# Attention scores from unsplit float32 operands, two heads on row halves, in place of split float32r products

## The chip, the cores and the metric

The kernel runs on one core of a Trainium2 chip. The metric is the device time of one execution in microseconds (us), the median of three runs. PE is TensorE, DVE is VectorE, ACT is ScalarE, POOL is GpSimd, SP is SyncE, which here only issues DMAs.

## What is computed

Attention with a soft cap, then two feed-forward networks, all in float32 from outside:

```python
# q, k, v: [2, 12, 448, 64]; cap = 30
scores = q @ k.T / 8
scores = cap * tanh(scores / cap)
attn = exp(scores - max(scores))
x = (attn / (sum(attn) + 1e-9)) @ v          # -> [896, 768]
h = x @ w_in                                 # [768, 2048]
x = max(0.01 * h, h) @ w_out                 # [2048, 768]
xn = x / sqrt(mean(x * x) + 1e-6) * rms_g
out = (silu(xn @ w_gate) * (xn @ w_val)) @ w_out2   # 768 -> 1536 -> 768
```

## The kernel before

The attention works on 12 pairs of heads (2 batches of 6 pairs). One tile `qk` of a pair holds, on 128 partitions, the 64 channels of both heads: 448 columns of queries (part "q"), 128 columns with the last 64 keys of both heads as two diagonal blocks (part "r"), and 384 columns with the first three blocks of 128 keys (part "k"). `scores` makes the scores of a pair in four units: the diagonal block "r" for both heads at once, with all 128 rows, and three units of one block of keys for each of the two heads. A head's keys and queries are on 64 partitions, so in these units each head uses one half of TensorE's rows.

Before, `split` gives `q` and `k` in two parts: `kqh` (float32r, rounded to 12 bits; cast on DVE, L453) and `kql = qk - kqh` (the helper at L345, on POOL, some on DVE). A score is then hi x hi + hi x lo + lo x hi. The first three pairs (0 to 2) do that with three products for each head, on row halves. For pairs 3 to 11 eight small DMAs on SP's queue (L478) also copy parts of both heads into `xq` and `xk`, so that hi x hi and lo x hi of a head are one product over all 128 rows (L509), and hi x lo stays a product on row halves (L499).

From the scores, ACT makes the tanh (L528) and the exponential (L536) into `e`. The weighted sums `weigh` are float32 products: one with all rows and columns (L547) for the last keys, then three units in which the two heads stand on halves of the columns (L550). For the denominator, `add_up` adds the blocks of `e` into `a` (L568 on DVE, L574 on POOL, then L581 for one head on POOL and for the other on DVE) and sums over the partitions on TensorE (L587, two float32 products on column halves). `finish` takes the reciprocal (L598), multiplies (L599) and splits the result into `xh` (L604, POOL) and `xl` (L345, DVE), the operands of the first network.

The order of instructions is written out beforehand. Every step is entered in a plan with an engine, an assumed cost in ns and a rank; the plan works through the steps in assumed time, takes on each engine the lowest rank among those that could start, and gives out the order found. Each engine then executes in that order and waits at semaphores where a step isn't ready. When TensorE has nothing ready in the plan, it gets a filler product (`warm`, L671, at most 18 calls). The 64-bit weights of the networks are decoded in the kernel into two float32r parts (`load_w`: DMA L380 on SP, ACT L383, DVE L387, L392 and twice L377, ACT L399, POOL or DVE L345); the first three blocks of `w_in` are decoded during the attention. The products of the first network (L710 for those blocks, then L795) can start when the last scores have been issued.

A step of TensorE's plan before, with its assumed cost, and the one of the weighted sums, which stays:

```python
plan.add("pe", (4 * MM, 0.75), r, across, reads, [(sc,)] + done)      # MM = 189 ns
...
plan.add("pe", 752 if i == 3 else 802, rank(h.n, "weigh"), product, reads, [(po,)])
```

Of the kernel before, what the change touches and what calls it, by code (L numbers as in the profile page):

```python
# [18 lines left out]
# Which engine does a step, how many buffers there are, and where kinds of steps stand (in hundredths of a pair)  # L19
# [3 lines left out]
    "kt": "2",  # L23
# [4 lines left out]
    "hk": "dve",  # L28
    "hq": "dve",
    "lk": "pool",  # L30
    "lq": "pool",
    "hk0": "dve",
    "hq0": "dve",
    "lk0": "pool",
    "lq0": "dve",
# [14 lines left out]
    "split": "-700",  # L50
    "low": "-130",
# [8 lines left out]
    "move": "-550",  # L60
    "load0": "-600",
    "load_v0": "-460",
    "split0": "215",
    "low0": "-670",
# [23 lines left out]
class Buf:  # L88
    """A tile that is taken from its pool where it is first written."""
# [15 lines left out]
class Fixed:  # L105
    """A tile that is there already."""
# [18 lines left out]
class Plan:  # L125
    """Steps with estimated costs, put in an order that keeps the engines busy."""
# [11 lines left out]
    def stretch(self, at, cost):  # L138
        """The time of a step of TensorE, whose clock is halved after a window with few matmuls."""
        cost, share, self.after = (*cost, 0) if isinstance(cost, tuple) and len(cost) == 2 else cost if isinstance(cost, tuple) else (cost, 1.0, 0)  # L140
        t = at
        while cost > 1e-6:
            tick = int((t + self.offset) / self.TICK + 1e-9)
            speed = 1.0 if self.seen.get(tick - 1, 0.0) >= self.ENTRY else 0.5
            step = min((tick + 1) * self.TICK - self.offset - t, cost / speed)
            self.seen[tick] = self.seen.get(tick, 0.0) + step * speed * 2.4 * share
            cost -= step * speed
            t += step
        return t - at
# [121 lines left out]
def softcap_attention_leaky_moe_gated_moe(  # L271
# [13 lines left out]
    """float32 products are carried as float32r pairs: x = hi + lo with hi = x rounded to 12 bits and  # L285
    lo = x - hi, which 12 bits hold exactly; x @ y = hi @ hi + hi @ lo + lo @ hi (+ lo @ lo where it
    rides along), every product exact and every sum in float32."""
# [27 lines left out]
    def scales():  # L315
        """|cap|, -|cap| and 1 / (|cap| sqrt(D))."""
        nc.vector.tensor_scalar_mul(ncap, cap_t, -1.0)
        nc.vector.tensor_max(acap, cap_t, ncap)
        nc.vector.reciprocal(tsc, acap)
        nc.vector.tensor_scalar_mul(tsc, tsc, SCALE)  # L320

    def network(ctx, bounded):
# [8 lines left out]
        def spare_w(i, part):  # L331
            """Room for one part of a block of a matrix in a spare block."""
# [17 lines left out]
        def load_w(src, hi=None, lo=None, rank=None):  # L350
            """A block of a float64 matrix (its words in src, [128, n]) as its two float32r parts.

            F, the upper word read as a float32, holds the upper eight exponent bits in its exponent; F * 2^-16
            moves the exponent's bias from float64's to float32's, the shift by three drops the sign and the
            exponent bits above float32's, and the three next bits of the fraction come from the lower word.
            Magnitudes outside of float32's range are clamped to it first."""
# [75 lines left out]
        def rank(n, kind):  # L432
            """Where steps of a kind for pair n stand among the steps that are ready."""
# [5 lines left out]
        def split(h):  # L439
            """q and k of a pair of heads, with the channels of both on the partitions, in their two parts."""  # L440
            raw, r = h.load["qk"], rank(h.n, "split")
            h.hi, h.lo = (Buf(st, [P, KW + QW], F32R, nm, 2) for nm in ("kqh", "kql"))
            alone = h.n < kn("n0", 2)
            for kind in ("q", "r", "k") if alone else ("q", "rk"):
                at = slice(parts_of[kind[0]].start, parts_of[kind[-1]].stop)
                n = at.stop - at.start
                eng = ENV["h" + kind + "0"] if alone else ENV["h" + kind[-1]]

                def upper(at=at, eng=eng):
                    if eng == "act":  # L450
                        nc.scalar.copy(h.hi[:, at], raw[:, at])
                    elif eng == "dve":
                        nc.vector.tensor_copy(h.hi[:, at], raw[:, at])  # L453
                    else:
                        nc.gpsimd.tensor_scalar(h.hi[:, at], raw[:, at], 1.0, 1.0, op0=ALU.mult, op1=ALU.mult)

                cost = {"act": cost_act(n), "dve": cost_dve(n, True), "pool": cost_pool(n, False)}[eng]
                plan.add(eng, cost, r, upper, [(raw, x) for x in kind], [(h.hi, x) for x in kind], [h.lo])
                eng = ENV["l" + kind + "0"] if alone else ENV["l" + kind[-1]]
                cost = {"dve": cost_dve(n), "pool": cost_pool(n, True)}[eng]  # L460
                plan.add(
                    eng, cost, rank(h.n, "low"),
                    lambda at=at, eng=eng: low(nc.vector if eng == "dve" else nc.gpsimd, h.lo[:, at], raw[:, at], h.hi[:, at]),
                    [(x, y) for x in (raw, h.hi) for y in kind], [(h.lo, x) for x in kind],
                )
            h.x = None
            if h.n < kn("n0", 2):
                return
            h.x = [Buf(st, [P, 2, m], F32R, nm, kn("xb", 2)) for nm, m in (("xq", KW), ("xk", 3 * P))]
            for j in range(2):  # L470
                own, other = (slice(i * D, (i + 1) * D) for i in (j, 1 - j))
                for i, (kind, to, src) in enumerate((("q", own, h.hi), ("q", other, h.hi), ("k", own, h.hi), ("k", other, h.lo))):
                    x = h.x[kind == "k"]
                    m = x.args[1][2]
                    at = slice(parts_of[kind].start, parts_of[kind].start + m)
                    plan.add(
                        "dma", [(650, 320 if kind == "q" else 274)], rank(h.n, "move"),
                        lambda x=x, to=to, j=j, src=src, own=own, at=at: nc.sync.dma_start(  # L478
                            x[to, j].bitcast(F32), src[own, at].bitcast(F32)
                        ),  # L480
                        [(src, kind)], [(x, j, i % 2)],
                    )

        def scores(h, at):
            """Some of the seven chunks of 128 keys: the soft cap of their scores, over |cap|."""
# [3 lines left out]
            stacked = h.x is not None and at[0] > 0  # L489
            hi, lo, queries = h.hi, h.lo, parts_of["q"]  # L490
# [5 lines left out]
            def products(terms, first, last):  # L496
                for m, (x, y) in enumerate(terms):
                    for j, rows in enumerate(rows_of):
                        nc.tensor.matmul(  # L499
                            sc[:, j, :S], x[rows, own], y[rows, queries],  # L500
                            start=first and m == 0, stop=last and m == len(terms) - 1,
                        )

            def across():
                xq, xk = h.x
                at = slice(c0 - parts_of["k"].start, c0 - parts_of["k"].start + P)
                products([(hi, lo)], True, False)
                for j in range(2):
                    nc.tensor.matmul(sc[:, j, :S], xk[:, j, at], xq[:, j], start=False, stop=True)  # L509

            done = [("scored",)] * (h.n == NPR - 1)
            share, r = 1.0 if at[0] == 0 else 0.5, rank(h.n, "score")
            if stacked:
                reads = [(hi, "k"), (lo, "q")] + [(x, j, k) for x in h.x for j in range(2) for k in range(2)]
                plan.add("pe", (4 * MM, 0.75), r, across, reads, [(sc,)] + done)
            else:
                terms = [(hi, hi), (hi, lo), (lo, hi)]
                groups = [(terms[:1], True, False), (terms[1:], False, True)] if h.n == 0 else [(terms, True, True)]
                for group in groups:
                    reads = {(x, kind) for x, _ in group[0]} | {(y, "q") for _, y in group[0]}  # L520
                    plan.add(
                        "pe", (len(group[0]) * len(rows_of) * MM, share), r,
                        lambda group=group: products(*group), sorted(reads, key=lambda v: (v[0] is lo, v[1])), [(sc,)] + done,
                    )
# [15 lines left out]
        def weigh(h, i):  # L540
            """One chunk of keys of each head: the heads are on halves of the columns, side by side."""
# [619 lines left out]
```

## Time and profile before

| | us |
|---|---|
| three runs | 645.37, 646.57, 647.38 |
| median | 646.57 |
| profiled execution, first to last instruction | 644.4 |
| TensorE busy in it | 619.7 (96%) |
| DVE busy | 493.3 (77%) |
| ACT busy | 270.5 (42%) |
| POOL busy | 240.7 (37%) |

Of the profiled execution only the span from its first to its last instruction is recorded; the timed runs lie 1.0 to 3.0 us above it. Busy time of TensorE is modelled, and its products overlap: the time from the start of one to the start of the next is the better measure of what a product costs. "Granted clock" is the share of full speed, 2.4 GHz, that TensorE's clock had.

### The profile page before, as it was taken

Reading aid. Unit: us, or ns where it says so; the run is one execution under the profiler, and the core shown is the slowest. Engines: PE = TensorE matmul, PEld = TensorE weight load, DVE = VectorE, ACT = ScalarE, POOL = GpSimd, SP = SyncE. Lnnn points to the kernel's source line nnn. Section 1 sums busy time; section 2 is a strip of 40 time slices with the busy share of each in tenths; the row PEclk is TensorE's granted clock in tenths of the full one; section 3 lists DMA queues with packets and bytes.
Section 4 is the critical chain, followed back from the end, with each engine's and each line's share of the span. In section 5 each row is a group of like instructions: output and inputs, shape, how many; then the busy total and the mean of one; then the engine's idle time right before and its main releaser. Section 6 shows DMA issues by size and latency. Waiting matters only on the chain.

```text
span 644.4 us, 7884 instructions
## 1 busy us (share of the span) xinstructions
PE 619.7 (96%) x2990; PEld 517.5 (80%) x2990; DVE 493.3 (77%) x577; ACT 270.5 (42%) x378; POOL 240.7 (37%) x150
## 2 busy tenths in 40 slices
PE   9988899999999999999999979999999999899996
PEld 6333333499999999998999869999999989899995
DVE  4999999989988885688866983998876269899110
ACT  6966777335545443333332442434333134333000
POOL 2867797612232222454353522333222034333100
PEclk9989999999999999999999989999999999999999
DMA  7566665122333323434344020343333022454110
GB/s 253 155 181 181 164 157 148 50 98 66 132 116 125 103 81 101 128 93 147 116 164 151 2 98 1 126 140 127 127 119 108 40 99 98 148 161 146 51 38 28
DMA packets 22719, 73.55 MB, mean 114 GB/s; under 512 B 3856, under 2 KB 10640, under 8 KB 22672
## 3 DMA queue, kind: packets, MB, share of 16 engines
q1 hardware_dynamic: 22672, 72.96, 35.8%
q8 instruction: 25, 0.41, 0.3%
q14 instruction: 22, 0.18, 0.1%
HBM read 62.52 MB, written 2.75 MB: 101 GB/s over the span
## 4 chain that ended last, share of the span: by engine, by line
PE 73%; DVE 14%; POOL 4%; DMA 3%; issue 3%; ACT 2%; SPq 1%; DVEq 0%; ACTq 0%; POOLq 0%
PE ps L795 32%; PE pt L795 15%; PE ps L840 15%; PE ps L1011 4%; DVE wm L377 3%; PE ps L888 3%; DVE rs L598 2%; PE sc L710 2%; DVE kqh L453 2%; DMA wraw<-in_moe_w_out_dram 2%; POOL kql L345 2%; DVE a L581 1%; DVE a L568 1%; PE pt L710 1%; DVE wm L387 1%
## 5 line engine op out<-in xcount | busy, mean ns | idle before, releaser
L377 DVE SCALAR_TENSOR_TENSOR wm<-wraw,wm 128x768 int32<-128x768 int32 (+1 forms) x140 | 168.4, 1203 | 2.8
L345 POOL TENSOR_TENSOR wlo<-wm,whi 128x768 fp32r<-128x768 f32 (+1 forms) x45 | 87.4, 1943 | 215.2 <-ACT whi L399 204.4
L383 ACT ACTIVATE wm<-wraw 128x768 f32<-128x768 f32 (+1 forms) x70 | 62.2, 889 | 127.3 <-DMA wraw<-in_moe_w_out_dram 54.9
L795 PE MATMUL ps<-low_g,whi 128*128 128x448 f32 x288 | 82.5, 367 | 0.0
L795 PE MATMUL ps<-low_g,spare 128*128 128x448 f32 (+1 forms) x330 | 67.7, 362 | 0.0
L387 DVE TENSOR_SCALAR wm<-wm 128x768 f32<-128x768 f32 (+1 forms) x70 | 44.4, 635 | 30.3 <-ACT wm L383 29.9
L795 PEld LDWEIGHTS ps<-low_g,spare 128*128 128x128 f32 x330 | 61.5, 188 | 4.6
L795 PEld LDWEIGHTS ps<-low_g,whi 128*128 128x128 f32 x288 | 54.1, 188 | 5.0
L795 PE MATMUL pt<-xl,whi 128*128 128x448 f32 x156 | 57.4, 368 | 0.0
L795 PE MATMUL pt<-xh,wlo 128*128 128x448 f32 x156 | 57.4, 368 | 0.0
L795 PE MATMUL pt<-xh,whi 128*128 128x448 f32 x156 | 57.4, 368 | 0.0
L345 DVE TENSOR_TENSOR high_g<-u,high_g 128x448 fp32r<-128x448 f32 x32 | 47.5, 1484 | 11.1 <-ACT high_g L641 9.7
L795 PE MATMUL ps<-low_g,wlo 128*128 128x448 f32 x144 | 53.1, 369 | 0.0
L528 ACT ACTIVATE e<-sc,tsc 128x896 f32<-128x896 f32 (+1 forms) x48 | 42.6, 910 | 21.6 <-PE sc L509 19.4
L392 DVE TENSOR_SCALAR wm<-wm 128x768 int32<-128x768 int32 (+1 forms) x70 | 46.8, 670 | 1.5
L399 ACT CAST whi<-wm 128x768 fp32r<-128x768 f32 (+1 forms) x45 | 36.4, 809 | 22.3 <-DVE wm L377 9.5
L840 PE MATMUL ps<-high_g,whi 128*128 128x448 f32 x152 | 43.6, 368 | 0.0
L840 PE MATMUL ps<-low_g,whi 128*128 128x448 f32 x152 | 43.6, 368 | 0.0
L536 ACT ACTIVATE e<-e,acap 128x896 f32<-128x896 f32 (+2 forms) x47 | 42.7, 957 | 0.0
L1072 DVE COPY o<-ps 128x384 f32<-128x384 f32 x14 | 7.6, 554 | 38.0 <-PE ps L795 38.0
L345 POOL TENSOR_TENSOR kql<-qk,kqh 128x448 fp32r<-128x448 f32 (+2 forms) x21 | 29.4, 1409 | 19.0 <-DVE kqh L453 18.6
L345 POOL TENSOR_TENSOR spare<-wm,spare 128x768 fp32r<-128x768 f32 x11 | 21.8, 1990 | 38.0 <-ACT spare L399 34.6
(154 smaller groups left out, 1232.2 us busy)
## 6 DMA issues: line engine op xcount, KB each, us to landing
wraw<-in_moe_w_out_dram SPq DMA_DIRECT2D x24, 768.0 KB, 4.5
wraw<-in_moe_w_in_dram SPq DMA_DIRECT2D x16, 768.0 KB, 4.4
wraw<-in_moe_w_gate_dram SPq DMA_DIRECT2D x12, 768.0 KB, 4.3
wraw<-in_moe_w_val_dram SPq DMA_DIRECT2D x12, 768.0 KB, 4.2
qk<-in_qk_dram SPq DMA_DIRECT2D x9, 480.0 KB, 4.0
xq<-kqh SPq DMA_DIRECT2D x36, 112.0 KB, 2.3
v<-in_v_dram SPq DMA_DIRECT2D x12, 256.0 KB, 2.8
wraw<-in_moe_w_out_dram SPq DMA_DIRECT2D x6, 512.0 KB, 3.6
```

Of the source, the lines that this page charges most:

```text
L345: eng.tensor_tensor(lo, x, hi.bitcast(F32), op=ALU.subtract)
L377: nc.vector.scalar_tensor_tensor(mi(), words(t), scalar, mi(), op0=op, op1=ALU.bitwise_or)
L383: lambda: nc.scalar.activation(m[:], upper(), AF.Abs, scale=2.0**-16), (raw,), (m,),
L387: lambda: nc.vector.tensor_scalar(m[:], m[:], W_MIN, W_MAX, op0=ALU.max, op1=ALU.min),
L392: lambda: nc.vector.tensor_scalar(mi(), mi(), 3, SIGN, op0=ALU.logical_shift_left, op1=ALU.bitwise_xor),
L399: ("act", 93 + n / 1.2, lambda: nc.scalar.copy(hi[:], shaped()), (m,), (hi,)),
L528: lambda: nc.scalar.activation(h.e[:, cs], sc[:, :n, :S], AF.Tanh, scale=tsc),
L536: lambda: nc.scalar.activation(h.e[:, at], h.e[:, at], AF.Exp, scale=acap),
L710: nc.tensor.matmul(to(), y[:, c], z, start=c == 0 and m == 0, stop=c == KD - 1 and m == 2,)
L795: nc.tensor.matmul(ps, a, m, start=n == 0, stop=n == 3 * len(terms) - 1)
L840: nc.tensor.matmul(sums[e, b], a[x][:, f - f0], m[y], start=f == 0 and i == 0, stop=f == KF - 1 and i == 2,)
L1011: nc.tensor.matmul(to[:], x[:, c], y, start=c == 0 and i == 0, stop=c == KD - 1 and i == 2)
```

## The change

The scores are now float32 products straight from the loaded tile `qk`: one full product for the block "r", and for each of the three other units one product for each head on its half of the rows. `split` is gone with its casts, subtractions and the eight moves of a pair, so `kqh`, `kql`, `xq` and `xk` are gone too. There are three `qk` tiles in place of two. The plan's assumed cost of a unit is 752 ns for "r" and 802 ns for the others. The ranks of the steps that stay are as they were. (The diff also empties comments and documentation strings.)

```diff
-    "kt": "2",
+    "kt": "3",
...
-        def split(h):
...
-                        nc.vector.tensor_copy(h.hi[:, at], raw[:, at])
...
-                    lambda at=at, eng=eng: low(nc.vector if eng == "dve" else nc.gpsimd, h.lo[:, at], raw[:, at], h.hi[:, at]),
...
-                        lambda x=x, to=to, j=j, src=src, own=own, at=at: nc.sync.dma_start(
-                            x[to, j].bitcast(F32), src[own, at].bitcast(F32)
-                        ),
...
-            def across():
-                xq, xk = h.x
-                at = slice(c0 - parts_of["k"].start, c0 - parts_of["k"].start + P)
-                products([(hi, lo)], True, False)
-                for j in range(2):
-                    nc.tensor.matmul(sc[:, j, :S], xk[:, j, at], xq[:, j], start=False, stop=True)
+            def products():
+                for j, rows in enumerate(rows_of):
+                    nc.tensor.matmul(
+                        sc[:, j, :S], qk_t[rows, own], qk_t[rows, parts_of["q"]], start=True, stop=True
+                    )
...
+            plan.add(
+                "pe", 752 if at[0] == 0 else 802, rank(h.n, "score"), products,
+                [(qk_t, kind), (qk_t, "q")], [(sc,)] + done,
+            )
...
-                    split(h)
```

## Rows read from the trace of the kernel before

**Rows 1.** Stages: length; busy us: PE, PEld, DVE, ACT, POOL; clock, DMA share, GB/s
```profile
0.00:13.80 13.80, 12.21 (x63) 8.97 (x64) 4.28 (x16) 8.34 (x10) 2.86 (x9) 1.00 0.84 281
13.80:126.70 112.90, 102.17 (x405) 42.70 (x404) 111.53 (x91) 81.37 (x96) 84.94 (x56) 0.98 0.56 149
126.70:242.00 115.30, 115.30 (x561) 105.14 (x561) 100.40 (x131) 55.51 (x90) 27.72 (x16) 1.00 0.30 101
242.00:644.40 402.40, 389.99 (x1967) 360.69 (x1965) 277.09 (x342) 125.26 (x183) 125.20 (x69) 0.99 0.31 102
```

**Rows 2.** PE's waits from 5.3 to 126.7 us: total us, times, longest
```profile
PE pt L587 <- DVE a L581: 5.9, 3, 3.1
PE pt L587 <- POOL a L581: 3.5, 4, 1.9
PE sc L499 <- DVE kql L345: 0.9, 1, 0.9
PE sc L499 <- ACT e L528: 0.3, 1, 0.3
```

**Rows 3.** PE in order of time: start us, length us, what, idle before
```profile
43.21 0.97 PE L587 MATMUL pt<-a,ones_f 128*64 128x448 f32 x2 [3.12 <-DVE a L581]
```

**Rows 4.** The stretch around it, columns as in rows 1
```profile
29.00:50.30 21.30, 18.18 (x69) 8.02 (x68) 21.10 (x17) 16.13 (x20) 15.78 (x11) 0.92 0.72 204
```

**Rows 5.** Stretch 13.8 to 126.7 us, instructions on kqh alone: PE, PEld, DVE, POOL
```profile
13.80:126.70 112.90, 25.94 (x114) 13.47 (x114) 12.70 (x23) 27.34 (x19) 0.98 0.56 149
```

**Rows 6.** Instructions of the tiles a and xl: ns min/median/max, first and last start
```profile
L568 DVE SCALAR_TENSOR_TENSOR a<-e,guard x12: 1134/1465/2167, 13.8 to 119.4; 128x896 f32<-128x896 f32 x12
L581 DVE TENSOR_TENSOR a<-a,e x12: 621/1410/1454, 19.3 to 124.4; 64x448 f32<-64x448 f32 x12
...
L345 DVE TENSOR_TENSOR xl<-t,xh x12: 555/1422/2525, 33.9 to 133.1; 128x448 fp32r<-128x448 f32 x12
```

**Rows 7.** PE in order of time: fillers and products of the next stage
```profile
7.53 0.71 PE L671 MATMUL pt<-ones_f,ident 128*128 128x128 f32 x4
...
28.36 0.94 PE L671 MATMUL pt<-ones_f,ident 128*128 128x128 f32 x6
...
115.46 0.47 PE L710 MATMUL sc<-xh,spare 128*128 128x448 f32 x1
...
122.53 0.47 PE L710 MATMUL sc<-xh,spare 128*128 128x448 f32 x1
...
125.30 1.45 PE L587 MATMUL pt<-a,ones_f 128*64 128x448 f32 x4
```

**Rows 8.** PE in order of time: score units and weighted sums
```profile
15.66 0.37 PE L499 MATMUL sc<-kqh 64*128 64x448 f32 x2
...
16.37 0.97 PE L550 MATMUL pt<-e,v 128*64 128x448 f32 x4
...
81.62 0.47 PE L499 MATMUL sc<-kql,kqh 64*128 64x448 f32 x2
...
82.62 0.47 PE L499 MATMUL sc<-kql,kqh 64*128 64x448 f32 x2
...
83.53 0.91 PE L547 MATMUL pt<-e,v 128*128 128x448 f32 x2
84.38 0.97 PE L550 MATMUL pt<-e,v 128*64 128x448 f32 x4
85.28 0.47 PE L499 MATMUL sc<-kql,kqh 64*128 64x448 f32 x2
...
86.19 0.37 PE L499 MATMUL sc<-kqh 128*128 128x448 f32 x1
...
86.90 0.97 PE L550 MATMUL pt<-e,v 128*64 128x448 f32 x4
...
113.05 2.48 PE L550 MATMUL pt<-e,v 128*64 128x448 f32 x12
```

**Rows 9.** Waits of SP's queue from 0 to 130 us: total us, times, longest
```profile
SPq L380 <- DVE wm L377: 34.1, 4, 19.9
```

More of the change, by code (lines that the diff above doesn't have):

```diff
@@ L27 @@
     "u": "5",
[L28 to L35, printed above, removed]
     "pt": "4",
@@ L49 @@
     "load_v": "175",
-    "split": "-700",
-    "low": "-130",
     "score": "-435",
@@ L59 @@
     "finish": "-165",
-    "move": "-550",
     "load0": "-600",
     "load_v0": "-460",
-    "split0": "215",
-    "low0": "-670",
     "score0": "-225",
@@ L437, in network @@
         parts_of = {"q": slice(0, KW), "r": slice(KW, KW + P), "k": slice(KW + P, KW + QW)}
-        def split(h):
[L441 to L452, printed above, removed]
-                        nc.vector.tensor_copy(h.hi[:, at], raw[:, at])
[L454 to L462, printed above, removed]
-                    lambda at=at, eng=eng: low(nc.vector if eng == "dve" else nc.gpsimd, h.lo[:, at], raw[:, at], h.hi[:, at]),
[L464 to L469, printed above, removed]
-            for j in range(2):
[L471 to L477, printed above, removed]
-                        lambda x=x, to=to, j=j, src=src, own=own, at=at: nc.sync.dma_start(
-                            x[to, j].bitcast(F32), src[own, at].bitcast(F32)
-                        ),
-                        [(src, kind)], [(x, j, i % 2)],
-                    )
@@ L487, in scores @@
             sc = Buf(ps_s, [P, 2, 512], F32, "sc", 2)
-            stacked = h.x is not None and at[0] > 0
-            hi, lo, queries = h.hi, h.lo, parts_of["q"]
+            qk_t = h.load["qk"]
             kind = "r" if at[0] == 0 else "k"
@@ L494, in scores @@
             rows_of = [slice(0, P)] if at[0] == 0 else [slice(j * D, (j + 1) * D) for j in range(2)]
[L496 to L502, printed above, removed]
-            def across():
-                xq, xk = h.x
-                at = slice(c0 - parts_of["k"].start, c0 - parts_of["k"].start + P)
-                products([(hi, lo)], True, False)
-                for j in range(2):
-                    nc.tensor.matmul(sc[:, j, :S], xk[:, j, at], xq[:, j], start=False, stop=True)
-            done = [("scored",)] * (h.n == NPR - 1)
[L512 to L524, printed above, removed]
+            def products():
[3 more added lines that the diff above has]
+                    )
+            done = [("scored",)] * (h.n == NPR - 1)
+            plan.add(
+                "pe", 752 if at[0] == 0 else 802, rank(h.n, "score"), products,
+                [(qk_t, kind), (qk_t, "q")], [(sc,)] + done,
+            )
             cs = slice(at[0], at[0] + n)
```

## Prediction

> **What bounds the kernel now.** I read four views in this order: the table of stages, TensorE's waits, TensorE's instructions in order of time, and the instructions of single tiles.
>
> The table of stages [rows 1] splits the run in two kinds. From 126.7 us on, the two feed-forward networks keep PE busy without a gap up to 242 us, and 390.0 of 402.4 us after that. Before 126.7 us is the attention; from 13.8 us on DVE works 111.5 of 112.9 us there, PE 102.2 with the clock granted at 0.98. The reader is to see that only the attention can give time back, and that what it gives arrives at the end nearly whole: the work behind it has no time of day of its own, PE simply starts it earlier.
>
> PE's waits in the attention [rows 2] come to 5.9 + 3.5 + 0.9 + 0.3 = 10.6 us, and 9.4 of them are one line: the sums over the partitions (L587), which wait for the additions of `a` on DVE and POOL (L581). PE takes its instructions in the order in which they were written out, so the scores behind such a wait are late too. The longest is 3.12 us, at 43.2 us [rows 3]. It also costs clock: in 29 to 50.3 us it was granted at 0.92 [rows 4], which is 0.08 x 21.3 = 1.7 us of full-speed work at most; I count 1.5. So DVE is the bound of the attention, and it reaches the end through L587.
>
> **What goes.** (1) In 13.8 to 126.7 us, work on the tile `kqh` (casts L453, some subtractions) takes 12.7 us of DVE and 27.3 us of POOL [rows 5]. All of it goes. (2) POOL and DVE hold each other up: with POOL at work DVE's L568 takes 1.47 us in the median and 1.13 at least, the subtraction into `xl` 1.42 against 0.56, L581 on DVE 1.41 against 0.62 [rows 6]. L581 on DVE runs beside its own half on POOL, which stays, so I expect nothing there. For the other two the excess is 12 x (1.465 - 1.134 + 1.422 - 0.555) = 14.4 us; POOL loses 27.3 of its 84.9 us [rows 1, 5], 0.32, so I take 4.6 us, with 0 and 14.4 as ends. DVE then needs 111.5 - 12.7 - 4.6 = 94.2 us after 13.8 us and is done at 108.0; without any relief at 112.6. (3) The 72 moves on SP's queue (8 for each of 9 pairs) go. They hold no engine themselves; the `v` and `qk` loads behind them come sooner. I price that at nothing: among PE's waits there is no load [rows 2], and loads that come sooner find PE busy. (4) The first 13.8 us: I expect no gain. The first tanh there needs the scale from `cap`, whose load no edit brings forward, and ACT has 8.3 us of work in them [rows 1].
>
> **What PE does in exchange.** First, PE's work now. From the first score (5.3 us) to the end of the last sum (126.7 us) are 121.4 us. In them lie the waits, 10.6; five groups of idle-time filler (L671), the first and last of them in [rows 7], 2.8 counted from start to next start; products of the next stage (L710) [rows 7], three at 115.5 us, 0.8 with their change of shape, and 2.8 from 122.5 to 125.3, 3.6; and the slow clock, 1.5. Left are 121.4 - 10.6 - 2.8 - 3.6 - 1.5 = 102.9 us of attention work, 8.6 a pair.
>
> A unit of scores (two blocks of keys) of pairs 3 to 11 is two products on row halves and two on all rows. Starts in [rows 8] give 82.62 - 81.62 = 1.00 us, and 83.53 - 82.62 = 0.91 when a full product follows; mean 0.95, 27 units. For pairs 0 to 2 it is three concurrent pairs of half products: 16.37 - 15.66 = 0.71 alone, about 0.60 inside a run, mean 0.65; 9 units. The block of the last 64 keys is three full products: 86.90 - 86.19 = 0.71, some 0.1 of it the change of shape; 0.60 to 0.71, 12 blocks.
>
> The new unit is two float32 products on row halves. No row shows that. The nearest are the weighted sums (L550), float32 on column halves: four records, 85.28 - 84.38 = 0.90 us alone, and three units in 115.46 - 113.05 = 2.41 us, 0.80 each, in a run. That row halves run together is seen at 15.66 us: two float32r products there take no longer than one full one. So 0.80 to 0.90; I take 0.87, since units will stand alone more often than in runs. The new last block is one full float32 product, as L547: 84.38 - 83.53 = 0.85. Sum: 27 x (0.87 - 0.95) = -2.2; 9 x (0.87 - 0.65) = +2.0; 12 x (0.85 - 0.60) = +3.0; in all +2.8. Ends: +0.3 (0.80 in every place) and +4.5 (0.90, and 0.90 for the block). PE then has 105.7 us of attention work (103.2 to 107.4).
>
> The Trainium skill (TensorEngine Tiling (Array Packing), Key Properties) says that a change of tiling mode drains TensorE. The 0.90 against 0.80 just read agrees with it. By that rule alone every new unit between others would pay the 0.10, and the sum would stand at its upper end, +4.5.
>
> **The sum.** The stretch less the foreign products is now 121.4 - 3.6 = 117.8 us. PE's new work alone is 105.7: 12.1 less. Of the filler, four groups with 1.9 us lie before 20 us, and 0.3 us of wait; there ACT sets the pace, so 2.2 us stay. That puts PE's end at 5.3 + 105.7 + 2.2 = 113.2 us, behind DVE's 108.0 to 112.6 and far behind ACT, whose 8.3 + 81.4 = 89.7 us [rows 1] fit. PE becomes the bound by a small margin. With DVE almost as full as PE some waits at L587 will stay: between none and 8 us; I take 2, since a chain that is ahead on average misses only at single places. Gain 12.1 - 2.2 - 2 = 7.9 us. The profiled span is 644.4 us; the median run, 646.57, lies 2.2 above it, and I take that margin as unchanged: 644.4 - 7.9 + 2.2 = 638.7; I say 638.5. The forecast's own range: best 117.8 - 103.2 - 1.0 = 13.6 gained, 633; worst 12.1 - 2.2 - 8 = 1.9, 644.7.
>
> **The rivals.** (A) *The row halves of a float32 product don't run together.* A float32 product shows as two records (L547 x2, L550 x4). If the second pass of head 0 must go before the first of head 1, a unit takes three passes of 0.85 / 2 in place of two: +0.42, x 36 = +15 us, and 646.6 - 9.9 + 15 = 651.7; if they run wholly one after the other, 1.70 - 0.87 = +0.83 x 36 = +30, 666.5. This ends on the other side: it decides from +0.27 us a unit on (9.9 / 36). For it: no row of float32 on row halves. Against it: both column halves of L550 in 0.90, hardly more than one full product (0.85). The Trainium skill (TensorE: Matmul & The Clock Gate, Part 3: Packing small matmuls — row/col tiling) says that matmuls start and end strictly in program order; if the passes stand head by head in that order, this is the first form. L550's 0.90 speaks against it for columns; no run here shows rows. Chance 0.09 (0.06 and 0.03).
>
> (B) *L587 goes on waiting.* The order of PE's queue is written from assumed costs; for DVE's L581 it is 65 + 448 / 0.96 = 532 ns, and the trace has 1.41 us [rows 6]. If the casts' time is only filled by the weight decoding that was pushed back, PE keeps 8 of its waits: gain 1.9 or less, 644.7. For it: DVE's 99% against a work that shrinks by only 15%. Against it: the weights to decode in this stage are three, a fixed amount. Chance 0.12.
>
> (C) *SP's queue holds loads back.* Its weight loads (L380) wait for DVE's decoding, 34.1 us in four waits [rows 9], and pair loads stand behind them. With the moves gone, loads and PE run closer to these waits. One of about 3.5 us on the path leaves a gain of 4.4: 642. Chance 0.06.
>
> (D) *The change does little because ACT binds.* It would need all of its 89.7 us plus gaps; 5.3 + 89.7 is 18 us short of PE's end. Chance 0.02, near 645.
>
> **How the numbers follow.** The forecast has 0.71. About 0.3%, 1.9 us, is what a measurement can tell from no change, so the borders are 644.6 and 648.5. Faster: 0.70 of the forecast, half of B (0.06), C (0.06): 0.82. Same: the rest of B, D and a little of the forecast: 0.08. Slower: A, and 0.01 for an order of instructions that is worse in a way not listed: 0.10. The range 632 to 645.5 holds the forecast with the cheap end of the unit, C, and most of B; A is left out with the far part of B.
>
> **What would show it.** Right: in the profile after, no work on `kqh`, `kql`, `xq`, `xk`; DVE below 95% between 14 and 112 us; the first product of the dense stage some 8 us earlier; PE's waits at L587 under 4 us; a unit of scores of four records in 0.80 to 0.90 us; the stage behind it of the same length. Wrong step by step: a unit over 1.2 us (A); L587 waits of 8 us or more (B); loads among PE's releasers (C); the clock below 0.98 in the attention, which would mean new gaps; or a dense stage that is longer than before by what the attention is shorter, since then DVE's decoding of the weights, and not PE, set its start.

## The result, and the profile after

The changed kernel takes 629.36 us in the median (four runs, 628.81 to 630.36); the kernel before took 645.97 beside it (645.29 to 647.38). The ratio is 0.9733, 95% interval 0.9715 to 0.9750. It is faster, but by 16.6 us where 7.9 were forecast, and the time lies below the range.

First the table of stages of the changed kernel, with the columns of [rows 1]. Its stages are cut where its own work changes: at 107.0 us, when PE has the first products of the dense stage, and at 224 us.

```profile
0.00:13.80 13.80, 12.34 (x50) 7.51 (x52) 0.69 (x5) 7.44 (x9) 0.85 (x7) 1.00 0.83 278
13.80:107.00 93.20, 90.63 (x369) 29.02 (x370) 80.77 (x66) 81.25 (x97) 53.16 (x37) 1.00 0.31 99
107.00:126.70 19.70, 19.70 (x97) 17.44 (x98) 16.82 (x23) 4.54 (x9) 2.62 (x3) 1.00 0.24 81
126.70:224.00 97.30, 97.30 (x482) 90.16 (x481) 82.47 (x109) 50.50 (x82) 27.23 (x14) 1.00 0.31 103
224.00:627.00 403.00, 391.04 (x1969) 361.73 (x1967) 278.68 (x343) 125.07 (x183) 126.82 (x69) 0.99 0.31 102
```

DVE was full in [rows 1] (111.5 of 112.9 us); now it works 80.8 of 93.2, and PE 90.6. The clock is at 1.00 throughout the attention. The last stage is as long as before (403.0 against 402.4). So the whole gain comes from ahead of it, and it does reach the end.

Next PE's waits up to 126 us (total, times, longest), against [rows 2].

```profile
PE pt L594 <- POOL ident masks.py:199: 1.5, 1, 1.5
PE sc L439 <- ACT e L451: 1.2, 1, 1.2
PE pt L510 <- POOL a L504: 1.2, 2, 0.6
```

The sums (L587, now L510) wait 1.2 us in place of 9.4, and never for DVE. L594 is a filler ahead of all work.

Then PE in order of time, against [rows 8]: start, length, instruction.

```profile
9.18 1.02 PE L439 MATMUL sc<-qk 64*128 64x448 f32 x4
10.14 0.49 PE L594 MATMUL pt<-ones_f,ident 128*128 128x128 f32 x2
...
31.84 1.77 PE L439 MATMUL sc<-qk 64*128 64x448 f32 x8
33.55 1.72 PE L473 MATMUL pt<-e,v 128*64 128x448 f32 x8
...
106.85 0.47 PE L632 MATMUL sc<-xh,spare 128*128 128x448 f32 x1
```

A unit of scores is four records. Two units stand at 31.84 us and the next work starts 33.55 - 31.84 = 1.71 later, 0.85 each; one alone at 9.18 takes 10.14 - 9.18 = 0.96. The row halves do run together. L632 (L710 before) starts at 106.85 in place of 115.46, 8.6 earlier.

Last the instructions of the tiles `a` and `xl` on DVE, against [rows 6] (ns, min/median/max).

```profile
L491 DVE SCALAR_TENSOR_TENSOR a<-e,guard x12: 1046/1147/1898, 14.9 to 102.0; 128x896 f32<-128x896 f32 x12
L504 DVE TENSOR_TENSOR a<-a,e x12: 622/623/1624, 18.3 to 108.1; 64x448 f32<-64x448 f32 x12
L332 DVE TENSOR_TENSOR xl<-t,xh x12: 610/622/626, 28.0 to 117.6; 128x448 fp32r<-128x448 f32 x12
```

All three came down to near their minima: 1465 to 1147, 1410 to 623, 1422 to 622. The middle one, the addition that the sums wait for, was expected to stay.

Where the time came from, by starts of PE's records: the first product of the first network's main loop (L795, now L717) starts at 129.9 us in place of 145.6, 15.7 earlier. That network's 468 products then take 94.9 us in place of 96.7, 1.9 less. Together 17.6, and the profiled span is 644.4 - 627.0 = 17.4 shorter.

### The profile page after: what moved, and what is told of

The parts are those of the page before. It is cut to its first block, busy times and chain, and to the rows that moved or that the text cites. A ratio compares the mean times of both kernels' runs of the same rounds, so it can differ in the third digit from the quotient of the medians.

```text
span 627.0 us, 7599 instructions
## 1 busy us (share of the span) xinstructions
PE 611.0 (97%) x2960; PEld 505.9 (81%) x2960; DVE 459.4 (73%) x544; ACT 268.8 (43%) x378; POOL 210.7 (34%) x129
## 4 chain that ended last, share of the span: by engine, by line
PE 85%; DVE 10%; DMA 1%; POOL 1%; issue 1%; ACT 1%; POOLq 0%; ACTq 0%; SPq 0%
PE ps L717 33%; PE pt L717 15%; PE ps L762 15%; PE sc L439 5%; PE ps L933 4%; DVE wm L364 4%; PE pt L473 3%; PE ps L810 2%; PE sc L632 2%; DMA wraw<-in_moe_w_out_dram 1%; PE pt L510 1%; PE pt L470 1%; PE pt L632 1%; PE pt L594 1%; DVE wm L374 1%
## 5 line engine op out<-in xcount | busy, mean ns | idle before, releaser
L717 PE MATMUL ps<-low_g,whi 128*128 128x448 f32 x288 | 82.5, 368 | 0.0
L717 PE MATMUL ps<-low_g,spare 128*128 128x448 f32 (+1 forms) x330 | 67.4, 361 | 0.0
L717 PEld LDWEIGHTS ps<-low_g,spare 128*128 128x128 f32 x330 | 61.5, 188 | 4.3
L717 PEld LDWEIGHTS ps<-low_g,whi 128*128 128x128 f32 x288 | 54.1, 188 | 5.0
L717 PE MATMUL pt<-xh,whi 128*128 128x448 f32 x156 | 57.0, 365 | 0.0
L717 PE MATMUL pt<-xh,wlo 128*128 128x448 f32 x156 | 57.0, 365 | 0.0
L717 PE MATMUL pt<-xl,whi 128*128 128x448 f32 x156 | 57.0, 365 | 0.0
L332 DVE TENSOR_TENSOR high_g<-u,high_g 128x448 fp32r<-128x448 f32 x32 | 44.5, 1391 | 12.4 <-ACT high_g L564 10.9
L717 PE MATMUL ps<-low_g,wlo 128*128 128x448 f32 x144 | 53.1, 369 | 0.0
L439 PE MATMUL sc<-qk 64*128 64x448 f32 (+1 forms) x168 | 47.2, 590 | 1.4 <-ACT e L451 1.2
L379 DVE TENSOR_SCALAR wm<-wm 128x768 int32<-128x768 int32 (+1 forms) x70 | 45.1, 645 | 1.5
L497 POOL TENSOR_TENSOR a<-a,e 128x896 f32<-128x896 f32 x12 | 25.9, 2155 | 43.1 <-DVE a L491 36.5
L439 PEld LDWEIGHTS sc<-qk 64*128 64x128 f32 (+1 forms) x168 | 15.7, 190 | 29.3 <-ACT e L451 15.4
```

The source lines that it names most:

```text
L332: eng.tensor_tensor(lo, x, hi.bitcast(F32), op=ALU.subtract)
L379: lambda: nc.vector.tensor_scalar(mi(), mi(), 3, SIGN, op0=ALU.logical_shift_left, op1=ALU.bitwise_xor),
L439: nc.tensor.matmul(sc[:, j, :S], qk_t[rows, own], qk_t[rows, parts_of["q"]], start=True, stop=True)
L497: lambda kind=kind: eng[kind].tensor_tensor(a[:], a[:], e[:, 5:7], op=ALU.add),
L717: nc.tensor.matmul(ps, a, m, start=n == 0, stop=n == 3 * len(terms) - 1)
```

## The experiments

The theory after the result: DVE held PE back through L587, as forecast, but PE lost far more by it than its waits show. The rivals: that a good part of the gain comes from the third `qk` tile, from the moves on SP's queue, or from the new order of instructions, which the plan works out anew whenever a step goes. The kernels were timed on more than one chip, so they are compared by their ratio to the kernel before on the same one; a difference of ratios is turned into time with 645 us.

**Parts of the change undone, with the plan free to reorder.** Four kernels put steps back into the changed kernel, as steps of the plan with their old ranks. The steps are dead (nothing reads their results), except in the last kernel, where the subtractions and moves read the casts and no product reads any of them; there everything but the products of the scores and their place in the plan is as before, with two `qk` tiles.

```diff
# e1_casts: the casts alone
+                plan.add(eng, cost, r, upper, [(raw, x) for x in kind], [(h.hi, x) for x in kind])
...
# e2_subs: subtractions of the same size and on the same engines
+                    lambda at=at, eng=eng: (nc.vector if eng == "dve" else nc.gpsimd).tensor_tensor(h.lo[:, at], raw[:, at], raw[:, at], op=ALU.subtract),
...
# e3_moves: the 72 moves alone, from qk
+                        "dma", [(650, 320 if kind == "q" else 274)], rank(h.n, "move"),
...
# e4_all: casts, subtractions and moves as they were
-    "kt": "3",
+    "kt": "2",
...
+                plan.add(eng, cost, r, upper, [(raw, x) for x in kind], [(h.hi, x) for x in kind], [h.lo])
...
+                    lambda at=at, eng=eng: low(nc.vector if eng == "dve" else nc.gpsimd, h.lo[:, at], raw[:, at], h.hi[:, at]),
...
+                        "dma", [(650, 320 if kind == "q" else 274)], rank(h.n, "move"),
```

> The kernel after with the DVE casts of the kernel before put back, into a tile that nothing reads; the scores stay float32. After has 80.8 us of DVE work in the 93.2 us from 13.8 to 107 us; the casts add about 15. Theory D (DVE was the bound, and its casts are what held TensorE up at the sums over the partitions): DVE is full again, +3 to +8 us. Rival P (POOL's subtractions did it, by holding POOL and slowing DVE): 0 to +1.5. Rival Q (SP's queue with its moves did it): 0. Rival S (the products of the scores themselves became cheaper on TensorE): 0.

> The kernel after with the subtractions of the kernel before put back on POOL (and the six small ones of the first pairs on DVE), of the loaded tile from itself, into a tile that nothing reads. POOL works 53 of 93 us in after; this adds about 27. Theory D: POOL stays under its limit and only slows some DVE instructions, +1 to +4 us. Rival P: +6 us or more. Rivals Q and S: 0.

> The kernel after with the 72 moves put back on SP's queue, from the loaded tile into tiles that nothing reads. Theory D: 0 to +1 us, since TensorE never waited for a load. Rival Q: +3 us or more. Rivals P and S: 0.

> The kernel after with casts, subtractions and moves all put back as they were in the kernel before and two loaded tiles in place of three, results unread; only the scores differ from the kernel before: float32 products from the loaded tile. Theory D: the whole gain is gone, 643 to 648 us. Rival S: the gain that came from the products stays, under 638 us.

| | median us | ratio to before | interval | over the changed kernel, us |
|---|---|---|---|---|
| e1_casts | 635.45 | 0.9860 | 0.9830 to 0.9890 | +8 |
| e2_subs | 634.73 | 0.9850 | 0.9817 to 0.9883 | +8 |
| e3_moves | 643.39 | 0.9983 | 0.9969 to 0.9996 | +16 |
| e4_all | 652.51 | 1.0141 | 1.0103 to 1.0178 | +26 |

The moves, which hold no engine, seemed to cost twice as much as the casts. That fits no theory of work, so the next question was what the order alone does.

**What the order is worth.** The same moves with a cost of nothing in the plan; the changed kernel with two `qk` tiles; the kernel before with a third `v` tile, and without the moves (all its pairs then use row halves); and the changed kernel with two `qk` tiles and the three weighted sums of a pair as one step.

```diff
# e7_moves_unplanned, against e3_moves
-                        "dma", [(650, 320 if kind == "q" else 274)], rank(h.n, "move"),
+                        "dma", [(0, 0)], rank(h.n, "move"),
# e5_two_tiles, against the changed kernel
-    "kt": "3",
+    "kt": "2",
# e6_before_v3, against the kernel before
-    "vb": "2",
+    "vb": "3",
# e8_before_no_moves, against the kernel before
-            h.x = [Buf(st, [P, 2, m], F32R, nm, kn("xb", 2)) for nm, m in (("xq", KW), ("xk", 3 * P))]
...
# e12_sums_together, against the changed kernel
-    "kt": "3",
+    "kt": "2",
...
-            plan.add("pe", 752 if i == 3 else 802, rank(h.n, "weigh"), product, reads, [(po,)])
+            plan.add("pe", 752 if i == 3 else 2410, rank(h.n, "weigh"), product, reads, [(po,)])
```

> As e3_moves, but the plan takes the 72 moves for free (0 ns of its queue), so that it writes out nearly the order of after; SP and the DMA engines still have to do them. If the order written out for a queue taken to be full is what cost the 14 us of e3_moves: 629 to 633 us. If the queue itself does it (its time, and loads that stand behind moves): 638 us or more.

> The kernel after with two loaded tiles in place of three. Theory K (the third tile carries a good part of the gain, since the tile is now held until the scores are through): +3 us or more over after. Theory D (DVE's relief carries it) and theory Q (SP's queue, free of the moves, carries it): 0 to +1.5 us.

> The kernel before with three tiles for the values in place of two, so that their loads need not stand so late among the moves. Theory Q (loads held up behind the moves cost time in the kernel before): 2 to 8 us less than before. Theory D: 0 to 1 us less.

> The kernel before without the moves: all twelve pairs make their scores as its first three do, three float32r products for each head on row halves. Casts and subtractions stay. Theory D: DVE is as full as before, so 641 us or more. Theory Q: 637 us or less. TensorE has less to do (0.65 in place of 0.95 us a unit), which by D alone gains nothing.

> The kernel after with two loaded tiles (626.0 us before, as e5) and the three units of weighted sums of a pair as one step of the plan, so that TensorE changes its shape less often. If TensorE's work bounds the attention now, 0.1 us saved at up to 24 places: 623.5 to 625.5 us. If the order written out matters more than that: anywhere from 622 to 634.

| | median us | ratio to before | interval |
|---|---|---|---|
| e7_moves_unplanned | 636.55 | 0.9889 | 0.9859 to 0.9918 |
| e5_two_tiles | 626.02 | 0.9725 | 0.9688 to 0.9762 |
| e6_before_v3 | 657.60 | 1.0201 | 1.0175 to 1.0226 |
| e8_before_no_moves | 658.76 | 1.0230 | 1.0206 to 1.0253 |
| e12_sums_together | 633.81 | 0.9829 | 0.9811 to 0.9847 |

The moves cost 16 us with their cost in the plan and 10 without it, in both cases the same moves. In e7_moves_unplanned the order on PE, ACT, DVE and POOL is that of the changed kernel, so its 10 us come from SP's queue: moves wait in it until their `qk` has landed, loads of `v` stand behind them, and PE waits for `v`. These are the waits of that queue and then of PE, up to 130 us (total, times, longest).

```profile
SPq L470 <- DMA qk<-in_qk_dram: 19.3, 7, 3.2
```

```profile
PE pt L520 <- DMA v<-in_v_dram: 8.1, 4, 2.9
```

A buffer more for `v`, no instruction more, makes the kernel before 13 us slower; without moves it is 15 slower. No theory had expected e4 above 648 us, or e6 slower than the kernel before. Where a step stands in the queues moves this kernel by nearly as much as the whole change, so none of the first four runs prices a part of the work.

The third tile brings nothing that can be measured: 0.9725 with two against 0.9733 with three. PE, ACT, DVE and POOL have the same instructions in the same order in both; only the loads on SP's queue differ. The trace shows a small loss at the start with three tiles, first the changed kernel, then the one with two tiles.

```profile
4.61 3.33 PE L439 MATMUL sc<-qk 128*128 128x448 f32 x6
```

```profile
4.61 1.92 PE L439 MATMUL sc<-qk 128*128 128x448 f32 x6
```

The first scores end 1.4 us later with three: the third pair's loads are issued among the first ones, and the 288 KB loads of these pairs land in 4.5 us (median) in place of 3.0. The lag is still 1.3 us at the end of the attention.

**The order held fixed.** Now the plan keeps every step of the kernel before, with its costs and ranks, and only what a step issues is changed. In the first kernel the casts, subtractions and moves issue nothing, and the scores are the new products; the plan goes on believing in two `qk` tiles, while four are real, as they are read longer. Three more give back casts, subtractions, or both; the last then differs from the kernel before by the products, the moves and the number of `qk` tiles alone.

```diff
# e9_old_plan_new_work, against the kernel before
-                plan.add(eng, cost, r, upper, [(raw, x) for x in kind], [(h.hi, x) for x in kind], [h.lo])
+                plan.add(eng, cost, r, lambda: None, [(raw, x) for x in kind], [(h.hi, x) for x in kind], [h.lo])
...
-                    lambda at=at, eng=eng: low(nc.vector if eng == "dve" else nc.gpsimd, h.lo[:, at], raw[:, at], h.hi[:, at]),
+                    lambda: None,
...
+                for j, rows in enumerate(rows_of):
+                    nc.tensor.matmul(sc[:, j, :S], qk_t[rows, own], qk_t[rows, queries], start=True, stop=True)
# e13_old_plan_casts (also in e15_old_plan_both), against e9
-                plan.add(eng, cost, r, lambda: None, [(raw, x) for x in kind], [(h.hi, x) for x in kind], [h.lo])
+                plan.add(eng, cost, r, upper, [(raw, x) for x in kind], [(h.hi, x) for x in kind], [h.lo])
# e14_old_plan_subs, against e9 (e15: low(...) as before)
-                    lambda: None,
+                    lambda at=at, eng=eng: (nc.vector if eng == "dve" else nc.gpsimd).tensor_tensor(h.lo[:, at], raw[:, at], raw[:, at], op=ALU.subtract),
```

> The order of instructions of the kernel before, with the work of the kernel after: the plan still counts casts, subtractions, moves and split products with their costs, but nothing is issued for the first three, and the scores are float32 products from the loaded tile. Every other instruction stands in the order of before. Theory W (the work that went is the gain, whatever the order): 627 to 634 us. Theory O (the order that the plan writes without that work is the gain): 641 us or more. Half and half: about 636.

> e9 (624.2 us: the order of before, the work of after) with the casts issued again where the plan has them, about 15 us of DVE, results unread. Theory C (the casts carry the gain, since DVE is what the sums wait for): 632 us or more. Theory P (the subtractions on POOL carry it): 624 to 627. If the two only bite together (either alone still leaves DVE room): 624 to 629 here and in e14, and 640 or more in e15.

> e9 with the subtractions issued again (27 us of POOL, 2.6 of DVE), of the loaded tile from itself, results unread. Theory C: 624 to 628 us. Theory P: 632 us or more. Together only: 624 to 629.

> e9 with casts and subtractions issued again as in the kernel before, results unread; it differs from the kernel before by the float32 products and the missing moves alone. If casts and subtractions are the whole of the change's effect: 641 to 647 us, the time of before. If the float32 products cost TensorE something that shows once it is not the bound: over 648. If the split products or the moves had cost time: under 639.

And the other way round, the order of the changed kernel with dead casts and subtractions riding along in the steps of the additions (e10 with the moves too, e11 without them):

```diff
# e10_new_plan_old_work, against the changed kernel (e11: no rider_moves)
+                lambda: (rider_dve(), nc.vector.scalar_tensor_tensor(a[:], e[:, 1:3], guard, e[:, 3:5], op0=ALU.add, op1=ALU.add)),
...
+                lambda kind=kind: (rider_pool(), eng[kind].tensor_tensor(a[:], a[:], e[:, 5:7], op=ALU.add)),
...
+                lambda: (nc.sync.dma_start(vt[:], v[b, hp].rearrange("p (c d) -> p c d", d=D)), n >= 3 and rider_moves(n)), [], [(vt,)],
```

> The order of after, with the work of before riding along: for each pair two casts on DVE ahead of the first addition, two subtractions on POOL ahead of the second, and, from pair 3 on, eight moves on SP behind the load of the values, all from a tile of constants into tiles that nothing reads; the plan doesn't know of them and nothing waits for them. About 10 us more on DVE, 31 on POOL, 72 moves. Theory W: 640 us or more. Theory O: 633 us or less.

> As e10, without the moves. Theory W with casts and subtractions as its main part: within 2 us of e10. Theory Q (the moves on SP's queue are the main part): at least 5 us under e10, near 631. Theory O: 633 us or less, as e10.

| | median us | ratio to before | interval | over e9, us |
|---|---|---|---|---|
| e9_old_plan_new_work | 624.18 | 0.9688 | 0.9666 to 0.9710 | |
| e13_old_plan_casts | 628.11 | 0.9747 | 0.9718 to 0.9777 | +3.8 |
| e14_old_plan_subs | 634.56 | 0.9840 | 0.9805 to 0.9874 | +9.8 |
| e15_old_plan_both | 643.45 | 0.9987 | 0.9973 to 1.0001 | +19.3 |
| e10_new_plan_old_work | 650.47 | 1.0091 | 1.0074 to 1.0108 | |
| e11_riders_no_moves | 650.12 | 1.0084 | 1.0067 to 1.0101 | |

So at a fixed order the casts and subtractions together carry the whole of the gain, 19.3 of 20.1 us. New products and moves together make 0.0013 x 645 = 0.8, not told from nothing. (The 1.9 us of the first network that stay open, below, would make the 19.3 to 21.2 and the 0.8 to -1.1.) The moves alone, e10 against e11, make 0.4, but there they copy constants and wait for nothing; e7 shows that moves cost something where a load that PE needs stands behind them. The riders of e11 cost 0.0351 x 645 = 22.6 us in the new order. The subtractions are worth more than the casts, and both together (19.3) more than their sum (13.6). The new work in the old order is the fastest kernel of the study, ahead of the changed one (0.9688 against 0.9733, intervals apart): the order that the plan makes after the change, with its third tile, costs about 3 us.

e9, e13, e14 and e15 have the same 528 products in the same order before the first product of the network's main loop, so its start measures what PE lost: 125.1 us in e9, 129.1, 136.1 and 144.9 in e13, e14 and e15. The next three fences are e14, with the subtractions, where the loss is 11.0 us (somewhat more than its time shows, for a reason that stays open, below): PE's waits, then the waits of PE's weight loads, then what waited for the tile `a`.

```profile
PE pt L589 <- DVE a L583: 3.2, 4, 1.3
```

```profile
PEld pt L589 <- DVE a L583: 8.3, 9, 2.1
...
PEld pt L589 <- POOL a L583: 1.1, 2, 0.7
```

```profile
PEld pt L589: 9.5, 11
PE pt L589: 3.2, 4
```

Of 11.0 us lost, PE's own waits show 3.2. The waits of the weight loads at the same line show 8.3 + 1.1 = 9.4. How a wait hides is to be seen in the order of time, e14 first, then e9 at the same products.

```profile
40.00 0.96 PE L589 MATMUL pt<-a,ones_f 128*64 128x448 f32 x2
41.37 0.97 PE L589 MATMUL pt<-a,ones_f 128*64 128x448 f32 x2 [0.40 <-DVE a L583]
42.27 1.97 PE L508 MATMUL sc<-qk 64*128 64x448 f32 x6
...
47.23 1.57 PE L589 MATMUL pt<-a,ones_f 128*64 128x448 f32 x4
48.72 1.02 PE L508 MATMUL sc<-qk 64*128 64x448 f32 x4
```

```profile
37.38 0.97 PE L588 MATMUL pt<-a,ones_f 128*64 128x448 f32 x4
38.28 1.97 PE L507 MATMUL sc<-qk 64*128 64x448 f32 x6
```

With `a` complete, the sums of both heads take 38.28 - 37.38 = 0.90 us, side by side on column halves. When one head's `a` comes late, its products run after the other's instead of beside them: 42.27 - 40.00 = 2.27 us, 1.37 lost, of which only 0.40 is marked as a wait; in the other 0.97 PE is busy with half of its columns. At 47.23 us the sums take 48.72 - 47.23 = 1.49 us and show no wait at all. In e15, too, PE's waits show only a part: 8.1 us of 19.8 lost.

```profile
PE pt L589 <- DVE a L583: 5.3, 4, 2.8
PE pt L589 <- POOL a L583: 2.8, 4, 1.7
```

Last, DVE's three steps in the first 140 us (busy us, mean ns), e9 and then e15.

```profile
L569 DVE SCALAR_TENSOR_TENSOR a<-e,guard 128x896 f32<-128x896 f32 x12 | 15.3, 1276 | 9.0 <-ACT e L537 8.9
L582 DVE TENSOR_TENSOR a<-a,e 64x448 f32<-64x448 f32 x12 | 10.5, 875 | 2.5 <-POOL a L575 2.2
L352 DVE TENSOR_TENSOR xl<-t,xh 128x448 fp32r<-128x448 f32 x12 | 10.2, 848 | 0.2
```

```profile
L570 DVE SCALAR_TENSOR_TENSOR a<-e,guard 128x896 f32<-128x896 f32 x12 | 19.1, 1593 | 5.3 <-ACT e L538 5.3
...
L352 DVE TENSOR_TENSOR xl<-t,xh 128x448 fp32r<-128x448 f32 x12 | 14.7, 1228 | 0.1
...
L583 DVE TENSOR_TENSOR a<-a,e 64x448 f32<-64x448 f32 x12 | 14.0, 1168 | 0.4
```

They fall from 19.1 + 14.7 + 14.0 = 47.8 us to 36.0, by 11.8. In e13, with the casts and no subtractions, they take 35.3; in e14, with subtractions and no casts, 47.8. The subtractions on POOL, not DVE's fuller queue, make them long.

How they do it can be seen at the shortest of the three, the addition that the sums wait for, in order of time: first the kernel before, behind a subtraction and behind the addition's own half on POOL, then e9 behind that half.

```profile
19.18 1.01 POOL L345 TENSOR_TENSOR kql<-qk,kqh 128x384 fp32r<-128x384 f32 x1 [0.35 <-issue]
19.27 1.39 DVE L581 TENSOR_TENSOR a<-a,e 64x448 f32<-64x448 f32 x1
...
26.66 1.33 POOL L581 TENSOR_TENSOR a<-a,e 64x448 f32<-64x448 f32 x1
27.04 1.45 DVE L581 TENSOR_TENSOR a<-a,e 64x448 f32<-64x448 f32 x1
```

```profile
69.92 1.13 POOL L582 TENSOR_TENSOR a<-a,e 64x448 f32<-64x448 f32 x1
70.81 0.73 DVE L582 TENSOR_TENSOR a<-a,e 64x448 f32<-64x448 f32 x1
```

DVE's addition ends 0.5 us after POOL's instruction in each: 20.66 after 20.19, 28.49 after 27.99, 71.54 after 71.05. In the kernel before, the changed one, e9, e13, e14 and e15 there are 72 such additions. The 30 that find POOL idle when they start take 0.62 us; the other 42 end 0.47 to 0.49 us after the end of a POOL instruction, whatever its work. So DVE does not slow down beside POOL here, it waits for POOL's instructions to end.

## Why the prediction was wrong, step by step

**Right.** What the attention gave back, 15.7 us, arrived at the end. DVE bound it through L587. The row halves run together (0.85 to 0.96 us a unit, forecast 0.87). The moves, where they stood, cost nothing that can be measured (with the new products 0.8 us, e15 against the kernel before). One sign came true by luck: the first product of the dense stage is 8.6 us earlier, as forecast (8), but before the change such products were put between the last ones of the attention, which went on to 126.7 us; the main loop behind them starts 15.7 earlier. Of the rivals, (A) fell with that unit. The Trainium skill (TensorE: Matmul & The Clock Gate, Part 3) has matmuls start and end in program order; whatever that means inside the two passes of a float32 product, the heads do not wait for one another here. (B) fell with 1.2 us of waits at the sums, (C) with no load among PE's releasers, (D) with PE busy 90.6 of 93.2 us and ACT 81.3.

**The step that failed** is PE's work now, "102.9 us of attention work, 8.6 a pair". It took the 10.6 us of PE's waits for all that PE lost, and so counted the rest of the loss as work, which the change then could not remove. In e9 PE does the new work and waits for nothing from 13.8 us on (its waits hold the filler ahead of all work and no other line):

```profile
13.80:126.70 112.90, 112.90 (x485) 50.88 (x485) 102.49 (x91) 87.09 (x110) 57.53 (x41) 1.00 0.27 94
```

By the starts of its records that work is 43.2 us of scores, 11.2 + 30.2 of weighted sums and 10.1 of sums: 94.7, 7.9 a pair, where the forecast had 105.7. In e15, the same products in the same order with casts and subtractions back, the same count gives 106.1 when every marked wait (8.1) is taken out. So 105.7 is what PE's records show while DVE and POOL hold it back, not its work. Of the difference of 11.4 the sums hold most, 17.0 against 10.1; the clock, granted at 0.92 from 29 to 50 us in e15 and at 1.00 in e9, can hold 0.08 x 21 = 1.7 at most. In the kernel before, the sums (L587) take 23.1 us, 5.9 of them marked waits between their own records: 17.2 again. The price of the exchange was about right: counted in this way the kernel before has 104.4, so the new products add 1.7, where 2.8 were forecast.

A better view was there before the change: the waits of the weight loads in the kernel before, 5 to 126 us.

```profile
PEld pt L587 <- DVE a L581: 12.2, 11, 3.9
...
PEld pt L587 <- POOL a L581: 6.6, 5, 2.6
```

18.8 us where PE's row has 9.4. In e13, e14 and e15 the losses were 4.0, 11.0 and 19.8 us; PE's rows at the sums show 0.6, 3.2 and 8.1, those of the loads 3.3, 9.4 and 18.1. A load's wait alone is no loss, though. In e9, where PE waits for nothing, the loads of the scores wait for ACT:

```profile
PEld sc L507 <- ACT e L529: 10.0, 15, 0.7
PEld sc L507 <- ACT e L537: 9.7, 15, 0.7
```

What tells is that the loads of the sums wait for `a`, which they never do in e9, and that single waits reach 3.9 us (0.8 at most in e9). The Trainium skill (Perfetto Trace Analysis, Optimization Strategy) advises to look for the gaps between an engine's slices and at what blocks there. On PE those gaps hold a third of the loss in e14, so that advice alone leads to the mistake made here.

The forecast's own sum, put beside the runs, in us (PE's end of the attention without the products of the next stage; the measured columns by starts of records):

| | forecast | e15, casts and subtractions back | e9, order of before | changed kernel |
|---|---|---|---|---|
| first score | 5.3 | 5.5 | 5.2 | 4.6 |
| PE's attention work | 105.7 | 106.1 | 94.7 | 97.3 |
| fillers and start | 2.2 | 2.8 | 2.8 | 3.4 |
| marked waits | 2 | 8.1 | 0 | 2.4 |
| end | 115.2 | 122.4 | 102.7 | 107.7 |
| gain against 123.1 | 7.9 | 0.7 | 20.4 | 15.4 |

**The second term, mis-sized:** DVE's relief by POOL was forecast at 4.6 us, with nothing for L581; it measured 11.8 between e15 and e9, of which L581 gave 3.5. "L581 on DVE runs beside its own half on POOL, which stays" failed as a reason: in the kernel before six of the 12 additions started behind that half and four behind a subtraction, while in e9 the half is still there but eight of 12 find POOL idle, and the median is 0.62 us. By the forecast's own sum, with 94.7 us for PE, a relief of 4.6 would have left DVE, at 108.0, the bound; so both terms had to be wrong for a gain of this size. The Trainium skill (SBUF — State Buffer, SBUF: two separate sides) describes a port that DVE and GpSimd share as a lock, which a DVE instruction with two inputs in SBUF and a GpSimd one that reads SBUF can't hold at once; the other waits for the whole instruction. The 42 additions that end behind POOL's instructions agree. So do the medians of the addition, 0.62 us in e9 and 1.33 in e14, and e13, where casts on DVE change nothing.

**Not foreseen:** the new order, which the forecast held at 0.01 for a worse one. It gives some 3 us back by the ratios, 5.0 us in the table above: 2.4 of waits, and 2.6 of PE's work. Of the 2.6, the scores hold 1.9, and 1.4 of these are the slow first ones with three tiles; weighted sums and sums hold 0.3 each. The two marked waits, 1.2 us for ACT and 1.2 at the sums, were not traced further; e12_sums_together, with fewer changes between shapes, was slower in all.

What stays open: the 468 products of the first network took 0.207 us each in the kernel before and in e1, e6, e9, e10 and e13, but 0.203 in the changed kernel and in the other experiments, at the same clock, in the one profiled execution of each; whether that belongs to the program or to the execution is not shown. That is 1.9 us of the gain, and no part of the change goes with it. Where e14 and e15 are set against e9, it makes their times look 1.9 us better.

## What to carry to other kernels

A wait on TensorE that is marked is a lower bound of what is lost: read the waits of its weight loads too, which can also be harmless, and compare the time from start to start of the same step where it waited and where it didn't. To price one edit in a kernel whose order is made by a planner, hold the order fixed and empty the steps, or the reordering is measured along with it (here up to 13 us from one buffer more). Work on GpSimd beside VectorE costs VectorE as well; look at the minimum and the median of the same instruction, and at what GpSimd is doing when it starts, before pricing that at little.

## What the runs showed of the hardware beyond what was expected

Float32 products of two heads on halves of the rows, 64 x 128 each over 448 columns, run together: 0.85 us for both in a run, 0.96 alone. Relief of DVE is not additive: casts on DVE cost 3.8 us and subtractions on POOL 9.8, both together 19.3. DVE looks full in each of them; what gives way first is the decoding of weights (15 of its first instructions, L384, by 140 us in e9, 13 in e13, 10 in e14 and in e15), and only in e15 is nothing more pushed back, though the subtractions are joined by the casts. That this is the reason is argued, not shown. Part of it can be the clock: of the four, only e15 had it below 1.00 (0.92 from 29 to 50 us), 1.7 us at most. And two kernels with the same products at the same granted clock can differ by 2% from start to start in a long run of matmuls, 1% in the length of a record, seen in one execution of each; these are the products of one line of the first network, before and then after (count, busy us, mean ns):

```profile
L795 PE MATMUL pt<-xh,wlo 128*128 128x448 f32 x156 | 57.4, 368 | 0.0
```

```profile
L717 PE MATMUL pt<-xh,wlo 128*128 128x448 f32 x156 | 57.0, 365 | 0.0
```
